# All of z by channel, half of the first expert weights loaded with the first pages, and work moved round the ends of the middle stages

## The chip, the cores and the metric

One Trainium2 chip, one core of it. The metric is device time in microseconds (us) for one execution of the whole program, as the median of the runs; the profile is of one execution of its own.

## What is computed

A long convolution with a computed filter, then a mixture of experts over every token of its result (float32 throughout):

```python
# x, v: (4, 10048, 128); pos_emb: (10048, 64)
h_filt = (np.maximum(pos_emb @ w1, 0) @ w2) * np.exp(-0.01 * pos)[:, None]
u  = x * v
Uf = np.fft.rfft(u, n=2 * S, axis=1)
Hf = np.fft.rfft(h_filt, n=2 * S, axis=0)
y  = np.fft.irfft(Uf * Hf[None], n=2 * S, axis=1)[:, :S]
x  = (x * y).reshape(B * S, D)                  # 40192 tokens of 128
# MoE: 4 groups of 4 experts, F = 1024; one group, then one expert, by argmax
g_idx = argmax(x @ w_group);  g_w = softmax(...)[g_idx]
e_idx = argmax(x[g_idx == g] @ w_expert[g]);  e_w = softmax(...)[e_idx]
out[token] = g_w * e_w * (np.maximum(x[token] @ w1[g, e], 0) @ w2[g, e])
```

## The kernel before

The transform is written as matrix products. A sequence is laid out as 128 positions by 79 (NB) blocks for each of the 128 channels (D). `dft_blocks` (L400) multiplies the folded input of three channels (`eo`) by a table and ScalarE (ACT) copies the result from PSUM to SBUF (L417) as the complex spectrum. That spectrum lives in two tiles: `z` holds the first 64 (KM) block frequencies, `zr` the other 15. In `z` the index order is [128, k, s, d] (s is the real or imaginary part, d the channel), in `zr` it is already [128, d, k, s]. Three steps use them:

- the *middle* of a batch, `middle` (L641) and `back` (L662), walks over the 79 frequencies two at a time (40 steps, k0 = 0, 2, ... 78): TensorE (PE) multiplies one frequency of all channels by a table (`dft_positions`, L489, result `psb`), VectorE (DVE) makes the two products with the filter's spectrum (`t0` L655, `t1` L658), GpSimd (POOL) adds and subtracts them into `y` (L656, L659), PE transforms back (L671, `pbp`), and ACT copies the result to `z` (L679) or `zr` (L682). `back` runs four steps (LAG) behind;
- the *next forward stage*, in which the inverse of the batch just done and the first transform of the next batch share one loop: PE transposes `zr` (L694, four channels in one) and `z` (L697, one channel each) through an identity, ACT copies the result (`tt`, L699), PE makes the inverse (L709, L730), DVE forms `yt` (L745) and `xy` (L747); beside them run `product` (L459), `fold` (L472) and `dft_blocks` (L406) of the next batch. `run_ahead` (L425) makes products and folds three parts (AHEAD) ahead of their use;
- at the end of the convolution a stage with the last inverse alone, whose `xy` is written into the space of `z`.

By the trace the stages are, in us: the filter to 119; the first transform of batch 0 to 175; middles at 175 to 249, 346 to 448, 553 to 658 and 772 to 875; shared stages at 249 to 346, 448 to 553 and 658 to 772; the last inverse to 945; then the choice of experts for the last batch and, from 969 to 2013, 164 pages of 256 tokens that each have one expert.

Tokens are sorted into pages as batches are done. For each batch, `chosen` (L800) computes the router's logits and the choice, and `ranked` (L857) counts (cnt L871, a small product pc on PE, L874), finds the page of every token and queues indirect DMAs on POOL: eight `clear`s (L387) of padding rows and 79 `put`s (L372) of tokens. Both are generators; the middle of the next batch calls them a step at a time (`next(routing)`), and the rest runs in the next shared stage. `scatter` (L324) sends queued clears and puts, a few for each step. A scheduler orders each engine's instructions, except that instructions marked `keep_in_program_order` stay as written, and `between`/`beyond` (L310, L317) hold POOL's indirect DMAs between marked POOL operations, here between one step's `y` L659 and the next.

In the ranking, four parts (h = 0 to 3) of 316 elements go through a scan, compares, a multiply by `dlt` (L960), an add (L963), a multiply by `oh` (L973) and a sum (L977). For batches 0 and 1, the three of h = 2 and 3 are on POOL (`w`, L956).

In the MoE part, each page loads its tokens (`xg`), and both halves of its expert's second weights (`ws`, L1236) from HBM. The first weights `m_w1` of all experts stay in SBUF as `mw0` and `mw1` (two halves of 4 MB); both are loaded in the last stage of the convolution, in 16 steps of 512 KB. `turn` (L1118) is one page's share of work: `high` (L1277) makes the high part of weights on ACT, `low` the rest, `first` (L1290) and `second` (L1310) are three products each, `leave` and `turn_back` bring the result to tokens (ys L1324, ptm L1331), `send` scatters it. What is left of `chosen` and `ranked` for the last batch runs beside the first pages.

## Time and profile before

| | us |
|---|---|
| runs, median (lowest to highest of 3) | 2032.28 (2028.17 to 2034.41) |
| the profiled execution, device time | 2026.35 |
| its span in the profile | 2024.4 |
| PE busy in the span | 1920.3 (95%) |
| DVE / ACT / POOL busy | 1607.3 / 1431.1 / 1302.2 |
| DMA, mean | 192 GB/s |

PE is busy nearly all the time, so a microsecond is to be had in two ways only: fewer or shorter PE instructions, or fewer of PE's idle stretches. The share of busy time is a mean over stages, so the stages are read one at a time, and PE's idle stretches are read with what ended them. The granted clock of PE (PEclk, 1.00 is 2.4 GHz, 0.50 is 1.2 GHz) is in the same rows. An fp32 product stands as two instructions in the trace (x4 is two frequencies), a transpose as one.

### The profile page before, as it was taken

What the parts mean: (1) busy time and instruction counts of PE and PEld (TensorE: products, weight loads), DVE (VectorE), ACT (ScalarE), POOL (GpSimd) and SP (SyncE); (2) the same over time, 40 slices, a digit from 0 to 9 for tenths busy, and PEclk for the clock granted to TensorE, in tenths of its full rate; (3) what the DMA queues carried; (4) which work ended last, traced back from release to release, by engine and by line L of the source; (5) the groups of instructions that cost most, each with busy time, mean ns of one, the idle gap of its engine ahead of it and who ended that gap; (6) DMA issues with size and microseconds to landing.
All of it is one profiled execution on the core that took longest, in us unless ns stands there. A gap on an engine that the chain in (4) does not pass through costs nothing.

```text
span 2024.4 us, 53259 instructions
## 1 busy us (share of the span) xinstructions
PE 1920.3 (95%) x17518; PEld 1768.2 (87%) x17518; DVE 1607.3 (79%) x3462; ACT 1431.1 (71%) x3395; POOL 1302.2 (64%) x1371
## 2 busy tenths in 40 slices
PE   8988999988998899988899999999999999999997
PEld 7867888767876787776799999999999999999997
DVE  5587766797669766883889998889999998888885
ACT  6663387427843585356787888888888888888886
POOL 3247700665798468966276777888888885555554
PEclk9999999989999899999899999999999999999999
DMA  4699967968998599877344445555555544443442
GB/s 140 213 270 259 291 178 210 334 191 224 278 333 262 159 249 342 287 249 257 107 147 143 143 152 147 158 192 157 163 157 157 161 142 127 133 130 124 123 124 67
DMA packets 258718, 388.72 MB, mean 192 GB/s; under 512 B 32679, under 2 KB 132754, under 8 KB 258432
## 3 DMA queue, kind: packets, MB, share of 16 engines
q1 hardware_dynamic: 225024, 317.84, 52.3%
q0 software_dynamic: 23904, 51.83, 7.3%
q10 hardware_dynamic: 9504, 15.54, 2.7%
q8 instruction: 142, 2.33, 0.5%
q14 instruction: 144, 1.18, 0.2%
HBM read 303.08 MB, written 83.04 MB: 191 GB/s over the span
## 4 chain that ended last, share of the span: by engine, by line
PE 70%; DVE 9%; issue 5%; DMA 4%; POOL 4%; ACT 4%; SPq 0%; ACTq 0%; DVEq 0%; POOLq 0%
PE py L1319 8%; PE py L1317 7%; PE py L1318 7%; PE ph L1298 7%; PE ph L1300 7%; PE ph L1299 7%; PE psb L489 6%; PE pbp L671 5%; PE psa L406 2%; PE po L730 2%; PE pt L697 2%; PE ptm L1331 2%; PE px L1255 2%; PE po L709 2%; PE ptr L812 2%
## 5 line engine op out<-in xcount | busy, mean ns | idle before, releaser
L1307 DVE SCALAR_TENSOR_TENSOR hl<-ph,hh 128x512 fp32r<-128x512 f32 x656 | 445.2, 684 | 93.3 <-ACT hh L1306 92.4
L1306 ACT ACTIVATE hh<-ph 128x512 fp32r<-128x512 f32 x656 | 393.8, 600 | 138.8 <-PE ph L1300 74.8
L372 POOL DMA_INDIRECT prow<-stg,adr x316 | 344.8, 1091 | 114.8 <-issue 54.8
L1343 POOL DMA_INDIRECT out<-os,to x328 | 344.8, 1051 | 91.5 <-issue 71.6
L1317 PE MATMUL py<-hh,wh 128*128 128x256 f32 x1312 | 399.4, 304 | 0.0
L1319 PE MATMUL py<-hh,wl 128*128 128x256 f32 x1312 | 373.9, 285 | 5.3 <-POOL wl L1287 5.3
L1298 PE MATMUL ph<-xh,wh 128*128 128x256 f32 x1312 | 374.3, 285 | 4.3 <-ACT wh L1280 2.5
L1300 PE MATMUL ph<-xh,wl 128*128 128x256 f32 x1312 | 374.0, 285 | 0.4 <-DVE wl L1287 0.4
L1299 PE MATMUL ph<-xl,wh 128*128 128x256 f32 x1312 | 373.8, 285 | 0.0
L1318 PE MATMUL py<-hl,wh 128*128 128x256 f32 x1312 | 371.8, 283 | 0.0
L1287 POOL TENSOR_TENSOR wl<-ws,wh 128x512 fp32r<-128x512 f32 x162 | 220.3, 1360 | 206.0 <-ACT wh L1280 205.0
L1319 PEld LDWEIGHTS py<-hh,wl 128*128 128x128 f32 x1312 | 252.0, 192 | 8.2 <-POOL wl L1287 8.2
L1298 PEld LDWEIGHTS ph<-xh,wh 128*128 128x128 f32 x1312 | 253.3, 193 | 5.0 <-ACT wh L1280 2.7
L1300 PEld LDWEIGHTS ph<-xh,wl 128*128 128x128 f32 x1312 | 253.5, 193 | 1.1 <-DVE wl L1287 0.8
L1299 PEld LDWEIGHTS ph<-xl,wh 128*128 128x128 f32 x1312 | 253.4, 193 | 0.1
L1318 PEld LDWEIGHTS py<-hl,wh 128*128 128x128 f32 x1312 | 253.4, 193 | 0.0
L1317 PEld LDWEIGHTS py<-hh,wh 128*128 128x128 f32 x1312 | 252.4, 192 | 0.0
L1287 DVE TENSOR_TENSOR wl<-mw,wh 128x512 fp32r<-128x512 f32 x328 | 236.7, 722 | 0.0
L656 POOL TENSOR_TENSOR y<-t 128x256 f32<-128x256 f32 (+1 forms) x160 | 119.7, 748 | 141.3 <-DVE t L655 135.7
L406 PE MATMUL psa<-fa,eo 96*64 96x158 f32 x2048 | 185.7, 310 | 23.2 <-DVE eo L472 11.2
L1280 ACT CAST wh<-mw 128x512 fp32r x328 | 205.8, 628 | 0.0
L1280 ACT CAST wh<-ws 128x512 fp32r<-128x512 f32 x328 | 204.7, 624 | 1.2 <-DMA ws<-m_w 1.2
(237 smaller groups left out, 4094.8 us busy)
## 6 DMA issues: line engine op xcount, KB each, us to landing
ws<-m_w SPq DMA_DIRECT2D x328, 256.0 KB
ht<-hspec SPq DMA_DIRECT2D x156, 256.0 KB
xv<-xv_in SPq DMA_DIRECT2D x131, 288.0 KB
bt<-c_b SPq DMA_DIRECT2D x95, 256.0 KB
xg<-prow SPq DMA_DIRECT2D x164, 130.0 KB
bp<-c_bp SPq DMA_DIRECT2D x76, 256.0 KB
stg<-xyd SPq DMA_DIRECT2D x76, 256.0 KB
xyd<-xy SPq DMA_DIRECT2D x57, 256.0 KB
```

The costliest lines, as they stand in the source:

```text
L372: ins = self.nc.gpsimd.indirect_dma_start(self.d["prow"], bass.IndirectOffsetOnAxis(ap=u.adr[:, t : t + 1], axis=0), u.rows[:, t - u.t0], ...
L1280: k.fix(k.nc.scalar.copy(hi, self.matrix(i, half, self.ea)))
L1287: ins = v.tensor_tensor(lo, self.matrix(i, half, self.ed), self.wh[i][half].bitcast(F32), ALU.subtract)
L1298: k.fix(nc.tensor.matmul(ph[:, j], wh, self.xh, start=True, stop=False))
L1299: k.fix(nc.tensor.matmul(ph[:, j], wh, self.xl, start=False, stop=False))
L1300: k.fix(nc.tensor.matmul(ph[:, j], wl, self.xh, start=False, stop=True))
L1306: k.fix(nc.scalar.activation(hh, ph, AF.Relu))
L1307: k.fix(nc.vector.scalar_tensor_tensor(hl, ph, 0.0, hh.bitcast(F32), ALU.max, ALU.subtract))
L1317: k.fix(nc.tensor.matmul(self.py, wh, self.hh[c], start=(c == 0), stop=False))
L1318: k.fix(nc.tensor.matmul(self.py, wh, self.hl[c], start=False, stop=False))
L1319: k.fix(nc.tensor.matmul(self.py, wl, self.hh[c], start=False, stop=(c == NC - 1)))
L1343: ins = k.nc.gpsimd.indirect_dma_start(k.d["out"], bass.IndirectOffsetOnAxis(ap=self.to[:, h : h + 1], axis=0), o[:, h], None, bounds_chec ...
```

## The change

- **Layout.** `z` becomes [128, d, k, s], as `zr` is. The transposes of `z` (L697) then read a channel's 128 values side by side instead of 512 bytes apart. `dft_positions` reads, for one frequency, pairs (s) that lie 512 bytes apart, instead of 256 values in a row. What it and `back` write to PSUM goes in the strided order that was used for `zr` only. ACT's copy of `dft_blocks` becomes contiguous on both sides.
- **Space.** The last batch's `xy` gets a tile of its own; `xo` has three buffers instead of four in the last stage.
- **Weights.** Only `mw0` is loaded in the last stage of the convolution. `mw1` is loaded in eight steps from MoE turn -2 on, and each of the first ten pages (EARLY) loads its own 256 KB of that half (`wf`).
- **Early products.** In the last four steps of a middle `run_ahead` makes four products and three folds of the next batch.
- **Later clears.** `scatter` in the middle no longer sends clears.
- **Ranking.** One more `yield` ahead of pc, for all but the last batch, and all of the ranking on DVE.

```diff
-        self.z = zp.tile([128, KM, 2, D], F32, name="z")
+        self.z = zp.tile([128, D, KM, 2], F32, name="z")
...
+        xyp = ctx.enter_context(tc.tile_pool(name="xy", bufs=1, reuse_waits="tile"))
         inner = ExitStack()
-        xyp = inner.enter_context(tc.tile_pool(name="xy", bufs=1, reuse_waits="tile"))
...
-                xy = self.z.rearrange("p k s d -> p (k s) d")[:, :NB]
-            elif b > 0:
+            if b > 0:
                 xy = xyp.tile([128, NB, D], F32, tag="xy", name=f"xy{b - 1}")
...
-                    self.scatter(i % 4 != 3)
+                    self.scatter(i % 4 != 3, False)
                     if i % 4 != 3 if i < 30 else i % 2:
                         next(routing, None)
+                    if i >= 36:
+                        self.run_ahead(b + 1, i - 36 - AHEAD - 1, made, folded)
...
-        return chain(*(self.moe_weights(pool, half) for half in range(2)))
+        return self.moe_weights(pool, 0)
...
-    def scatter(self, n):
+    def scatter(self, n, clear=True):
...
+            elif not clear:
+                break
...
-                self.by_channel(k0, ps)[:, i],
+                ps[:, i].rearrange("p s d -> p d s"),
                 bt[:, i],
-                self.frequency(k0 + i),
+                self.frequency(k0 + i, 1)[:, :, 0],
...
-                    src = self.z[:, :, :, d0 + s + i].rearrange("p k s -> p (k s)")
+                    src = self.z[:, d0 + s + i].rearrange("p k s -> p (k s)")
...
         yield
+        if b < self.nbat - 1:
+            yield
         pc = self.psr([128, 2, NE], "pc")
...
-            w = v if b >= self.nbat - 2 or h < 2 else nc.gpsimd
...
-            w.tensor_tensor(lt, lt, bc(dlt[:, es], 2, NB), ALU.mult)
+            v.tensor_tensor(lt, lt, bc(dlt[:, es], 2, NB), ALU.mult)
...
+        self.weights = self.moe_weights(
+            right.enter_context(tc.tile_pool(name="second", bufs=1, side="right", reuse_waits="tile")), 1
+        )
...
         p3.begin()
+        next(self.weights, None)
...
+        if self.q < EARLY:
+            self.wf = k.sp.tile([128, 512], F32, tag="wf", name="wf", bufs=3)
+            src = k.d["m_w1"][:, ds(es, 1), 512:1024]
+            k.tc.keep_in_program_order(nc.sync.dma_start(self.wf, src.rearrange("p e f -> p (e f)")))
...
+        if half and self.q < EARLY:
+            return self.wf
```

Three places show how the order of work moves. In the rows a name's number tells its buffers apart. The first place is the end of batch 1's middle (about 428 to 448 us in the trace of before), on POOL. Of before, from the first half of the last step's `y` on; `empty` to `prow` is a clear, and `y<-t1` is L659:

```order
L656 TENSOR_TENSOR y_5724<-t0_5725 128x128
L387 DMA prow<-empty_81,fidx_5548 13056x520
L659 TENSOR_TENSOR y_5636<-t1_5640 128x2x128
L387 DMA prow<-empty_81,fidx_5548 13056x520
L659 TENSOR_TENSOR y_5678<-t1_5682 128x2x128
L387 DMA prow<-empty_81,fidx_5548 13056x520
L659 TENSOR_TENSOR y_5706<-t1_5710 128x2x128
L387 DMA prow<-empty_81,fidx_5548 13056x520
L659 TENSOR_TENSOR y_5724<-t1_5728 128x128
```

Of after, the last three steps on POOL (after's line numbers: `y` is L657 and L660, a clear L391):

```order
L657 TENSOR_TENSOR y_5672<-t0_5673 128x2x128
L660 TENSOR_TENSOR y_5672<-t1_5676 128x2x128
L657 TENSOR_TENSOR y_5701<-t0_5702 128x2x128
L660 TENSOR_TENSOR y_5701<-t1_5705 128x2x128
L657 TENSOR_TENSOR y_5722<-t0_5723 128x128
L660 TENSOR_TENSOR y_5722<-t1_5726 128x128
L391 DMA prow<-empty_81,fidx_5584 13056x520 x8
```

The clears have moved behind the last `y`. On DVE at the same place, of before, the last two steps' products and the first rows of the ranking behind them:

```order
L655 TENSOR_TENSOR t0_5707<-psb_5703,ht_5697 128x512
L896 CAST npg_5524<-ni_5528 128x16
L658 TENSOR_TENSOR t1_5710<-psb_5703,ht_5697 128x512
L912 SCALAR_TENSOR_TENSOR end_5525<-ones_2987,used_68,npg_5524 128x16
L922 TENSOR_SCALAR lastp_5540<-npg_5524 128x16
L655 TENSOR_TENSOR t0_5725<-psb_5722,ht_5720 128x256
L913 TENSOR_TENSOR start_5534<-end_5525,npg_5524 128x16
L923 TENSOR_SCALAR lastp_5540<-lastp_5540 128x16
L658 TENSOR_TENSOR t1_5728<-psb_5722,ht_5720 128x256
L914 TENSOR_SCALAR base_5535<-start_5534 128x16
```

Of after on DVE, the end of what now stands ahead of those two steps (the block of 49 rows begins with the cast of npg, right behind t1_5676), and the two steps:

```order
L955 TENSOR_TENSOR lt_5683<-lt_5683,dlt_5624 128x316
L463 TENSOR_TENSOR xv_5686<-xv_5686 96x3x128
L476 TENSOR_TENSOR eo_5689<-xv_5664 96x384
L656 TENSOR_TENSOR t0_5702<-psb_5698,ht_5692 128x512
L659 TENSOR_TENSOR t1_5705<-psb_5698,ht_5692 128x512
L463 TENSOR_TENSOR xv_5712<-xv_5712 96x3x128
L476 TENSOR_TENSOR eo_5715<-xv_5686 96x384
L656 TENSOR_TENSOR t0_5723<-psb_5720,ht_5718 128x256
L659 TENSOR_TENSOR t1_5726<-psb_5720,ht_5718 128x256
L958 TENSOR_TENSOR f_5640<-f_5640,lt_5683 128x316
```

The ranking, which stood between and behind the last two steps' products, now stands ahead of them, with the early products of the next batch (`xv`, `eo`) among them. The second place is the same spot in batch 2's middle, where it is the same with 64 rows. The third is the start of the MoE part on DVE. Of before, the choice of experts of the last batch ahead of page 0's `hl` (L1307):

```order
L768 TENSOR_TENSOR ohe_14337<-dfe_14331,mxe_14329 128x64
L786 SCALAR_TENSOR_TENSOR smg_14030<-smg_14030,sme_14339 128x16
L791 TENSOR_TENSOR oh_13094<-ohe_14337,ohg_14028 128x16x16
L787 RECIPROCAL en_13095<-smg_14030 128x16
L760 TENSOR_REDUCE mxg_14641<-lg_13498 128x15
L762 TENSOR_TENSOR dfg_14643<-lg_13498,mxg_14641 128x60
L765 SCALAR_TENSOR_TENSOR dfg_14643<-dfg_14643,order_2996 128x60
L770 TENSOR_REDUCE smg_14651<-exg_14645 128x15
L766 TENSOR_REDUCE mxg_14641<-dfg_14643 128x15
L768 TENSOR_TENSOR ohg_14649<-dfg_14643,mxg_14641 128x60
L778 TENSOR_TENSOR pr_14653<-lg_13498,ohg_14649 128x240
L1307 SCALAR_TENSOR_TENSOR hl_13799<-ph_13785,hh_13798 128x512
```

Of after, the first piece of the same work between two `hl` and a `wl` of the pages:

```order
L1312 SCALAR_TENSOR_TENSOR hl_13666<-ph_13658,hh_13665 128x512
L777 TENSOR_REDUCE le_14334<-pr_14030 128x64
L754 TENSOR_REDUCE mxe_14336<-le_14334 128x16
L756 TENSOR_TENSOR dfe_14338<-le_14334,mxe_14336 128x64
L1292 TENSOR_TENSOR wl0_13673<-wf_13618,wh0_13669 128x512
```

What stood in one piece of 21 rows ahead of `hl` is split there into four pieces with pages' work between them.

## Rows read from the trace of the kernel before

**Rows 1.** Busy time by stage (columns in the first line; x is instructions).

```profile
core 0: us, PE busy (x) PEld busy (x) DVE busy (x) ACT busy (x) POOL busy (x), PEclk, DMA share, GB/s
249.00:346.00 97.00, 95.53 (x1441) 84.02 (x1442) 65.22 (x123) 81.15 (x215) 0.79 (x2) 1.00 0.67 183
...
346.00:448.00 102.00, 94.75 (x577) 75.61 (x577) 81.89 (x196) 40.05 (x93) 68.28 (x91) 0.95 0.87 283
...
448.00:553.00 105.00, 96.64 (x1440) 85.13 (x1440) 75.85 (x147) 81.80 (x214) 65.31 (x71) 0.97 0.85 233
...
658.00:772.00 114.00, 104.86 (x1422) 90.36 (x1422) 82.16 (x173) 80.94 (x210) 65.84 (x72) 0.91 0.78 214
...
875.00:945.00 70.00, 60.27 (x932) 51.95 (x930) 43.00 (x107) 46.47 (x87) 45.04 (x46) 1.00 0.81 274
...
969.00:1070.00 101.00, 94.36 (x742) 93.53 (x742) 89.43 (x224) 79.66 (x181) 53.89 (x48) 0.93 0.43 131
```

**Rows 2.** The weight loads of the transposes of z: group by line, count, busy us, mean ns.

```profile
L697 PEld LDWEIGHTS pt<-ident,z 128*128 128x128 f32 x512 | 82.3, 252 | 16.6 <-ACT tt L699 14.4 <-issue 2.0
```

**Rows 3.** PE in time, four transposes each (start us, us, work, count).

```profile
249.83 0.75 PE L697 MATMUL pt<-ident,z 128*128 128x128 f32 x4
...
952.46 0.60 PE L812 MATMUL ptr<-ident,z 128*128 128x128 f32 x4
```

**Rows 4.** PE in the first middle: psb and pbp, k0 below 64, then from 64.

```profile
215.11 1.03 PE L489 MATMUL psb<-z,bt 128*128 128x256 f32 x4
215.97 1.02 PE L671 MATMUL pbp<-y,bp 128*128 128x256 f32 x4
...
234.12 1.04 PE L489 MATMUL psb<-zr,bt 128*128 128x256 f32 x4
235.00 1.02 PE L671 MATMUL pbp<-y,bp 128*128 128x256 f32 x4
```

**Rows 5.** psb by group: count, busy us, mean ns of one.

```profile
L489 PE MATMUL psb<-z,bt 128*128 128x256 f32 x640 | 161.0, 385 | 9.5 <-DMA bt<-c_b 5.2 <-DVE hs L630 2.2 <-ACT zr L417 0.6
...
L489 PE MATMUL psb<-zr,bt 128*128 128x256 f32 x150 | 41.9, 402 | 0.6 <-DVE hs L630 0.4
```

**Rows 6.** PE in time at the end of batch 1's middle and after.

```profile
428.02 0.40 PE L874 MATMUL pc<-cnt,tri 128*128 128x16 f32 x2 [1.78 <-DVE cnt L871]
...
435.02 0.60 PE L489 MATMUL psb<-zr,bt 128*128 128x256 f32 x2
...
440.58 6.92 PE L671 MATMUL pbp<-y,bp 128*128 128x256 f32 x18 [4.96 <-POOL y L659]
...
459.16 1.06 PE L406 MATMUL psa<-fa,eo 96*64 96x158 f32 x6 [5.61 <-DVE eo L472]
```

**Rows 7.** POOL there: the first clear, and its wait.

```profile
438.68 1.08 POOL L387 DMA_INDIRECT prow<-empty,fidx  x1 [1.79 <-DVE oh L950]
```

**Rows 8.** DVE there: a t of the last step but one, and the next folds.

```profile
434.41 0.69 DVE L655 TENSOR_TENSOR t<-psb,ht 128x512 f32<-128x512 f32 x1 [0.27 <-POOL y L656]
...
458.56 1.95 DVE L472 TENSOR_TENSOR eo<-xv 96x384 f32<-96x384 f32 x4
```

**Rows 9.** Busy time while DVE ranks there.

```profile
436.77:447.13 10.36, 6.55 (x18) 5.24 (x18) 10.36 (x41) 1.80 (x4) 7.63 (x9) 0.67 0.58 187
```

**Rows 10.** A wait of PE at 658 to 772 (us in total, times, longest).

```profile
PE psa L406 <- DVE eo L472: 5.6, 2, 4.9
```

**Rows 11.** Multiply by dlt in the ranking, on POOL and on DVE.

```profile
L960 POOL TENSOR_TENSOR lt<-lt,dlt 128x316 f32<-128x316 f32 x4 | 4.3, 1081 | 6.6 <-DVE cur L1044 3.9 <-DVE lt L957 2.6
...
L960 DVE TENSOR_TENSOR lt<-lt,dlt 128x316 f32<-128x316 f32 x12 | 6.0, 503 | 0.0
```

**Rows 12.** The start of the MoE part: PE's wait, and 985 to 1005 us.

```profile
PE ptm L1331 <- ACT ys L1324: 4.0, 1, 4.0
...
985.00:1005.00 20.00, 16.02 (x115) 15.82 (x113) 18.57 (x51) 14.97 (x34) 7.17 (x7) 0.83 0.25 78
```

**Rows 13.** SP's queue at the first page.

```profile
971.33 2.59 SPq L1236 DMA_DIRECT2D ws<-m_w  x4
```

## What the change should do to the time

> **What bounds the kernel now.** I read the busy time by stage first [rows 1]. PE is busy 95.53 of 97 us in the first shared stage at a granted clock of 1.00, and from 92 to 93% in the middle of batch 1 and in two of the later shared stages; the last inverse is the loosest of the convolution's stages (60.27 of 70). So PE bounds nearly every stage, and each change is priced by what it takes off PE's own work or off PE's idle stretches. DVE is next (81.89 of 102 in a middle); ACT has slack there (40.05 of 102). Then I read what ended PE's idle stretches: at the end of a middle POOL's `y`, 4.96 us [rows 6]; in the stage behind it the folds `eo` on DVE, 5.61 us [rows 6], and 5.6 us again a batch later [rows 10]; at the start of the MoE part 4.0 us for `ys` [rows 12]. After such stretches the granted clock is under 1: 0.67 in 436.77 to 447.13 [rows 9], 0.91 over the stage from 658 [rows 1], 0.83 in 985 to 1005 [rows 12]. Below 1.00 a part of the stage ran at 1.2 GHz, so a gap costs more than its length.
>
> **Layout, the transposes.** There are 512 transposes of `z` [rows 2], 128 in each of four stages. Four of them take 0.75 us, and four whose source is contiguous take 0.60 [rows 3]: (0.75 - 0.60) / 4 = 0.0375 us each, 512 x 0.0375 = 19.2 us of PE, 4.8 us in each stage. What of it reaches the end: three of the stages are bound by PE for 92% and more of their time, and there I take 80%, 3 x 3.8 = 11.5 us, because ACT (81.15 of 97) and DVE stand close behind. In the last inverse PE idles 14% of the time, and I take half, 2.4 us. Together **-14 us**. Bounds: -19 (all of it) and -8 (half of the three, nothing of the last).
>
> **Layout, the products.** `psb` for k0 below 64 now reads pairs 512 bytes apart. The nearest row is `psb` from `zr`, which reads such pairs 128 bytes apart: 1.04 us for four against 1.03 [rows 4]. That is 2.5 ns each, x 640 instructions [rows 5] = +1.6 us. By group means it is 402 against 385 ns [rows 5], +10.9 us, but these durations overlap in the pipeline, so four in a row is the better reading. I take **+2**; bounds 0 and +11, and what the longer distance might add is a rival below. `back` writes PSUM strided in both cases: 1.02 against 1.02 [rows 4], 0. ACT's copies to `z` become runs of four values; ACT has 62 idle us in the middle of batch 1 [rows 1] to hide any growth. Without that cover, one copy later per step would reach PE only through the transposes at the stage's end: 0 to +1.
>
> A sentence of the Trainium skill (SBUF — State Buffer, the note on "cachelines" at the end of the part Door 1) speaks against this change: any non-contiguous access to PSUM slows matmuls significantly. It gives no figure to put in the sum. Both `psb` and `pbp` now write so for every k0, 128 more instructions per stage and kind. Rows 4 show the same pattern already, from k0 = 64 on, at 0.01 us for four; so the row decides, and the sum holds nothing for it.
>
> **Later clears and early products, end of batch 1's middle.** Before: PE ends the last `psb` at 435.02 + 0.60 = 435.62, then waits 4.96 us and needs 6.92 us for 18 `pbp` [rows 6]. Four take 1.02 us, about 0.22 each [rows 4], so 18 are 4 us of work in 11.9 us: 8 us lost. The cause is POOL: the first clear stands ahead of the last four `y` and waits 1.79 us for its list, which DVE makes in the ranking [rows 7]. After that comes the 5.61 us for the folds, which DVE makes only when it is through with that ranking (458.56 in [rows 8]). The change takes the clears out of there. But the order of DVE shows that it puts a block of 49 rows of ranking ahead of the products t0, t1 of the last two steps, so the wait is not gone, it changes hands: PE now waits for DVE. The price: such a stretch holds 41 instructions in 10.36 us, DVE full [rows 9]. Some of these are long only beside POOL's clears (I estimate 2 us), the block holds a product and a fold more of about 0.5 us each (1.95 us for four [rows 8]); I take 9 us, bounds 8 and 11. The t1 ahead of the block ends at about 434.0 (t0 of the next step starts at 434.41 in [rows 8], after a short wait that goes with the clears); the block then ends at 443.0. Two pairs of products (0.69 us each for a full step [rows 8], half that for the last) and two more early rows make 3 us, POOL's two halves of the last `y` and one `pbp` 1 us: PE ends the middle at 447 instead of 447.5. So the tail itself gives -0.5. The early folds are there when the next stage wants them, which takes away the 5.61 us; but the ranking that remains on DVE is longer (below), and I leave 2 us of waiting. Sum **-4**, bounds +1 (block 11 us and the wait back for half) and -10 (block hidden behind early `psa`).
>
> **The same for batch 2.** The block has 64 rows, by the same price per row about 11 us, where before the ranking stood behind the products: I take the tail 2.5 us longer. In the stage behind, the waits of 5.6 us for folds go [rows 10], and with them some of the time at 1.2 GHz (0.91 [rows 1]: if that stands for half speed in 18% of 114 us, 20 us ran slowly). Against it, DVE has the rest of the ranking. **-1.5**, bounds +4 and -12. For the middle of batch 3 the order stays: 0.
>
> **Ranking on DVE.** For batches 0 and 1, twelve instructions go from POOL to DVE; the multiply is 503 ns there against 1081 [rows 11]. At about 0.5 to 0.6 us each, six per batch are +3 us of DVE's time. The stage from 346 and those behind it have DVE at 66 to 80% [rows 1]; this is in the 2 us that I left above, and the next bound would be +3 each if DVE were full there. The added `yield` delays the count by one call, but PE's order around pc is the same in all three batches: its wait of 1.78 us [rows 6] stays, 0.
>
> **Weights, and the start of the MoE part.** In the last inverse SP issues eight loads of 512 KB fewer; DMA there is at 0.81 of its time [rows 1], PE waits for DVE and ACT, so 0. In the pages 4 MB more and ten times 256 KB come over about 100 us that move 131 GB/s now, 67 GB/s more; other stages move 283 [rows 1], so there is room. The first page: `wf` is the third load on SP's queue behind two `ws`, which takes 2.59 / 4 = 0.65 us per issue [rows 13], so it is asked for 1.3 us after the first `ws`, and the cast of it stands in ACT's queue ahead of `hh` of the next page; I charge +2.5 (bounds 0 and +8, the two first pages each waiting out a load). The gain here is not in the weights: the order of DVE splits the choice of experts of the last batch, which stood in one piece of 21 rows ahead of `hl`, and for which PE waits 4.0 us [rows 12]. Without it 4 us go, and of 20 us at a clock of 0.83 (34% of them at half speed, 3.4 us lost) I take 2. **-3.5** in all, bounds -8 and +8.
>
> **Space.** The own `xy` and one `xo` buffer less: `xo` is loaded by SP ahead of need, and the eight mw loads that shared the queue are gone, 0 to +2; taken as 0.
>
> **The sum.** -14 + 2 - 4 - 1.5 - 3.5 = -21. The profiled execution took 2026.35 us on a span of 2024.4; it gives 2005.35. It lies 5.93 under the median of 2032.28, and I forecast on the median: 2032.28 - 21 = **2011.3 us**. With all good halves of the small terms 2004, with the bad ones 2018.
>
> **Rivals.** First, *the distance of 512 bytes is what costs*, not the single hit in a line. For it: the old transposes are the only row that jumps 512 bytes, and they are the slow ones. Against it: `zr`'s pairs run at nearly full rate, but at 128 bytes. Then each `psb` pays for 128 jumps what a transpose pays, 37.5 ns, x 640 = 24 us, less the 2 in the sum: 2033, no change. If every value pays, it is twice that, +48: 2057, slower. It decides at 23 us, 36 ns for each of 640 instructions.
>
> The same note of the Trainium skill (SBUF — State Buffer, "cachelines") speaks against this rival: it counts hits in a line of 16 bytes, not the distance, and two in a line are enough for the full rate. By it the +2 of `psb` would be 0 and the time 2009; the trace agrees for pairs at 128 bytes [rows 4], and no row before shows pairs at 512.
>
> Second, *all waits go*: DVE's block hides behind the early `psa`, the stage behind batch 2 stays at full clock, the transposes give all 19: -19 + 2 - 10 - 12 - 7 = -46 at the most; half of the excess over my sum gives 1998 and all of it 1986. For it: PE does have early `psa` in its order there. Against it: these stand behind the `pbp` that wait.
>
> Third, *the wait only changes hands and the first pages pay*: the ends of the middles give nothing (0 and +4), `wf` and the mw1 loads put ahead of the tokens' loads in SP's order cost +7 at the first pages: -14 + 2 + 0 + 4 + 3.5 = -4.5: 2028; with milder terms 2020. For it: the DVE order. Against it: the bandwidth in hand.
>
> **How the numbers follow.** The forecast (2004 to 2018) has a chance of 0.55, the second rival (1986 to 2004) 0.17, the third (2018 to 2029) 0.17, the first 0.11: 0.05 at no change, 0.06 slower. A measurement of this kernel tells about 0.3%, 6 us, from no change, so faster begins below 2026.2: 0.55 + 0.17 + 0.12 = 0.84; same 0.05 + 0.05 = 0.10; slower 0.06. The range from 1994 to 2029 leaves out the lower half of the second rival and the first, 0.08 + 0.11 = 0.19.
>
> **What would show it.** Right: four transposes of `z` at 0.60 us; four `psb` below k0 = 64 at 1.04; no wait of PE for POOL's `y` at the end of batch 1's and 2's middles but one for t0 or t1 on DVE of 5 to 9 us; no 5.6 us wait for `eo`; no 4.0 us wait for `ys` at the MoE start, but 1 to 3 us for a `wh` or `wl` of `wf`. Wrong: `psb` at 1.15 us or more for four (first rival); stages behind the middles that lose what the tails gain; first pages that wait for `xg` or `ws`.

## The result

The changed kernel takes 2008.15 us (median of 4 runs, 2007.0 to 2012.78), the kernel before, beside it, 2031.82; the ratio is 0.990 (95% interval 0.9878 to 0.9922). By the two medians that is 23.7 us less, by the ratio some 20; I forecast 21 less and 2011.3 us. The profiled execution took 2008.12 us on a span of 2005.9.

The profile after, the busy time by stage; the columns are those of [rows 1], a stage starts with PE's first instruction of it:

```profile
core 0: us, PE busy (x) PEld busy (x) DVE busy (x) ACT busy (x) POOL busy (x), PEclk, DMA share, GB/s
247.00:339.50 92.50, 89.17 (x1431) 76.99 (x1430) 63.41 (x120) 76.92 (x210) 0.49 (x1) 1.00 0.67 184
339.50:443.80 104.30, 96.50 (x598) 75.78 (x596) 84.95 (x210) 41.62 (x98) 64.20 (x87) 0.95 0.84 274
443.80:540.10 96.30, 89.04 (x1425) 76.52 (x1423) 71.38 (x140) 77.49 (x211) 64.66 (x67) 1.00 0.91 252
540.10:654.60 114.50, 99.40 (x596) 75.34 (x596) 94.34 (x225) 41.76 (x98) 95.25 (x121) 0.93 0.84 280
654.60:750.10 95.50, 91.40 (x1429) 78.37 (x1427) 75.06 (x155) 77.29 (x210) 57.01 (x62) 0.98 0.91 252
853.30:923.50 70.20, 58.03 (x933) 48.19 (x934) 42.27 (x105) 44.95 (x87) 45.80 (x45) 0.98 0.69 214
946.50:1028.30 81.80, 77.66 (x611) 76.12 (x612) 73.91 (x182) 66.02 (x149) 44.81 (x40) 0.94 0.69 223
```

The first three shared stages (247, 443.8 and 654.6) have become shorter, the middles between them longer, above all the one from 540.1. Read the same way in both traces, from the first `psb`, the first transpose of `zr` or the first `px` to the next, and within the MoE part from a page's first `ptm`, the stages compare so (us; a negative difference is a gain):

| stage | before | after | difference |
|---|---|---|---|
| filter, then transform of batch 0 | 119.2 + 55.9 | 116.5 + 54.9 | -3.7 |
| middle 0, shared stage 1 | 73.8 + 97.0 | 75.6 + 92.6 | -2.6 |
| middle 1, shared stage 2 | 102.2 + 105.1 | 104.2 + 96.3 | -6.7 |
| middle 2, shared stage 3 | 104.0 + 115.9 | 114.5 + 95.5 | -10.0 |
| middle 3, last inverse, choice | 101.6 + 94.6 | 103.2 + 93.2 | +0.2 |
| pages 0 to 10 | 85.2 | 81.7 | -3.5 |
| pages 40 to 80 | 251.8 | 257.8 | +6.0 |
| other pages | 718.2 | 719.8 | +1.7 |

The sum is -18.6 us, 5 us less than the medians differ: the profiled execution of before (2026.35) lay that much under its median, and the one of after did not. So the table tells where the time went, and the medians how much it is in all.

The layout does in PE's rows what was forecast. Transposes of `z`, and `psb` and `pbp` in the first middle (compare [rows 3] and [rows 4]); columns: start, us, work, count:

```profile
211.17 1.03 PE L493 MATMUL psb<-z,bt 128*128 128x256 f32 x4
212.04 1.02 PE L669 MATMUL pbp<-y,bp 128*128 128x256 f32 x4
...
247.36 1.47 PE L691 MATMUL pt<-ident,z 128*128 128x128 f32 x12
...
450.87 1.04 PE L691 MATMUL pt<-ident,z 128*128 128x128 f32 x8
```

Twelve transposes take 1.47 us and eight 1.04, so one more costs (1.47 - 1.04) / 4 = 0.108 us. `psb` over pairs 512 bytes apart takes 1.03 us for four, as before: no loss at all. All transposes of `z` together, of before and of after (count, busy us and mean ns, then PE's idle time ahead of them):

```profile
L697 PE MATMUL pt<-ident,z 128*128 128x128 f32 x512 | 94.0, 322 | 6.5 <-ACT tt L699 6.5
L691 PE MATMUL pt<-ident,z 128*128 128x128 f32 x512 | 72.3, 280 | 14.3 <-ACT tt L693 14.1
```

PE is busy with them for 21.7 us less, and waits 7.6 us longer for ACT's copies `tt`. With the old layout in the changed kernel (the first experiment) it is 93.1 us and 6.5 us of waits, so both come from the layout.

The end of batch 1's middle, first PE, then DVE and POOL (compare [rows 6] to [rows 8]; the bracket is idle time ahead of the instruction and what ended it):

```profile
428.87 0.60 PE L493 MATMUL psb<-zr,bt 128*128 128x256 f32 x2
429.31 2.75 PE L669 MATMUL pbp<-y,bp 128*128 128x256 f32 x12
437.52 1.84 PE L410 MATMUL psa<-fa,eo 96*64 96x158 f32 x10 [5.46 <-DVE eo L476]
439.93 3.16 PE L669 MATMUL pbp<-y,bp 128*128 128x256 f32 x6 [0.56 <-POOL y L660]
...
427.99 0.24 DVE L892 CAST npg<-ni 128x16 f32<-128x16 int32 x1
...
436.92 0.55 DVE L476 TENSOR_TENSOR eo<-xv 96x384 f32<-96x384 f32 x1
437.39 0.68 DVE L656 TENSOR_TENSOR t<-psb,ht 128x512 f32<-128x512 f32 x1
...
438.15 0.72 POOL L657 TENSOR_TENSOR y<-t 128x256 f32<-128x256 f32 x1 [9.26 <-DVE t L656]
```

The clears are gone from between the `y`, and the block of ranking has come in their place: it starts at 427.99 on DVE and ends at 437.47, 9.5 us (I took 9), PE waits 5.46 us, and POOL 9.26 for the next `t`. A batch later it is the same with the longer block: its first and last rows on DVE, and PE's wait.

```profile
632.86 0.76 DVE L892 CAST npg<-ni 128x16 f32<-128x16 int32 x1
...
646.40 0.56 DVE L476 TENSOR_TENSOR eo<-xv 96x384 f32<-96x384 f32 x1
...
PE psa L410 <- DVE eo L476: 9.2, 2, 9.0
```

That block takes 14.1 us, where I took 11.

### The profile page after: what moved, and what is told of

Same layout as the page of the kernel before. It is cut to its first block, busy times and chain, and to the rows that moved or that the text cites. A ratio compares the mean times of both kernels' runs of the same rounds, so it can differ in the third digit from the quotient of the medians.

```text
span 2005.9 us, 53303 instructions
## 1 busy us (share of the span) xinstructions
PE 1896.0 (95%) x17518; PEld 1733.8 (86%) x17518; DVE 1624.4 (81%) x3478; ACT 1417.9 (71%) x3395; POOL 1303.4 (65%) x1355
## 4 chain that ended last, share of the span: by engine, by line
PE 64%; DVE 10%; DMA 6%; POOL 6%; ACT 4%; issue 4%; SPq 0%; ACTq 0%; DVEq 0%; POOLq 0%
PE py L1324 7%; PE ph L1303 7%; PE py L1322 7%; PE ph L1305 7%; PE py L1323 7%; PE ph L1304 7%; PE psb L493 5%; PE pbp L669 4%; PE po L724 2%; PE ptm L1336 2%; PE px L1258 2%; DMA xv<-xv_in 2%; PE ptr L806 2%; PE po L703 1%; DMA v<-xv_in 1%
## 5 line engine op out<-in xcount | busy, mean ns | idle before, releaser
L1322 PEld LDWEIGHTS py<-hh,wh 128*128 128x128 f32 x1312 | 251.7, 192 | 0.0
L657 POOL TENSOR_TENSOR y<-t 128x256 f32<-128x256 f32 (+1 forms) x160 | 121.6, 760 | 157.1 <-DVE t L656 154.2
L1285 ACT CAST wh<-mw 128x512 fp32r x318 | 199.9, 629 | 0.0
```

Source lines behind the costliest of these rows:

```text
L1285: k.fix(k.nc.scalar.copy(hi, self.matrix(i, half, self.ea)))
L1322: k.fix(nc.tensor.matmul(self.py, wh, self.hh[c], start=(c == 0), stop=False))
```

## The experiments

Each kernel is told as an edit of the changed kernel, or of the kernel before where it says so. The medians are read beside the runs of before on the same chip. The kernels came to several chips: before took 2031.82 us beside the changed kernel, 2030.23 beside the first four edits and 2033.49 beside the next four, so a difference of medians from two of these groups holds up to 3 us of the chips, and the ratio of each of these eight to before is known to 3 to 5 us. The last four (the ranking on DVE alone and those below it) ran on chips on which the kernel before took 2114 and 2125 us, so of them only ratios and single rows of undisturbed places are used.

**The old layout of z.**

```diff
-        self.z = zp.tile([128, D, KM, 2], F32, name="z")
+        self.z = zp.tile([128, KM, 2, D], F32, name="z")
...
-                    src = self.z[:, d0 + s + i].rearrange("p k s -> p (k s)")
+                    src = self.z[:, :, :, d0 + s + i].rearrange("p k s -> p (k s)")
```

> The changed kernel with the old layout of z ([128, k, s, d]) and everything else as changed. Theory of the prediction: the layout is the largest term, so this is 13 to 18 us slower than the changed kernel (2021 to 2026 us), four transposes of z take 0.75 us again, four psb below k0 = 64 stay at 1.03, and the filter and first transform, which came out 3.7 us shorter with no term in my sum, get that back because the copies from psa are strided again. Rival: most of the gain came from the waits at the ends of the middles, and the transposes only uncover other waits; then this is at most 6 us slower (2014 or less).

Measured: 2017.6 us, 0.9944 of before (0.9924 to 0.9964); the changed kernel is 9.5 us faster by medians. That lies between the theory (13 to 18) and the rival (6 or less). Its windows of the three shared stages and the last inverse, and PE's largest wait in the last inverse:

```profile
251.10:347.10 96.00, 94.32 (x1432) 83.13 (x1431) 63.67 (x120) 80.45 (x210) 0.46 (x1) 1.00 0.65 179
451.40:548.50 97.10, 94.15 (x1425) 82.63 (x1423) 71.37 (x140) 80.57 (x211) 64.44 (x67) 1.00 0.90 252
663.30:761.00 97.70, 95.68 (x1429) 83.94 (x1427) 75.28 (x155) 80.44 (x210) 58.59 (x62) 0.99 0.89 246
864.70:935.00 70.30, 63.38 (x939) 54.85 (x940) 42.82 (x104) 46.54 (x88) 44.70 (x45) 0.98 0.69 213
...
PE pt L701 <- ACT tt L703: 3.1, 7, 0.5
```

In stage 1 PE does 5.2 us less in the changed kernel (89.17 against 94.32), and the stage is 3.5 us shorter (92.5 against 96.0): 70% come through. In stage 2 PE does 5.1 us less and the stage is 0.8 us shorter, in stage 3 4.3 less and 2.2 shorter: 16% and 50%, each from one pair of traces. In the last inverse PE does 5.4 us less (58.03 against 63.38) and the stage is as long (70.2 against 70.3): nothing comes through. There the changed kernel's PE waits longer for ACT's copies of the transposes and for `yt`:

```profile
PE pt L691 <- ACT tt L693: 4.9, 7, 0.7
PE po L703 <- DVE yt L739: 2.6, 3, 1.5
```

The filter and the first transform are not explained by the layout: kernels whose work there is that of the changed one came to the transform of batch 0 at 116.5 to 119.8 us, which spans the 119.2 of before. So the -3.7 of the table lies within the spread between executions and can't be told from it. By these traces the layout is worth 3.5, 0.8 and 2.2 us in the three shared stages; where the rest of the 9.5 us lies isn't shown.

**No early products.**

```diff
-                    if i >= 36:
-                        self.run_ahead(b + 1, i - 36 - AHEAD - 1, made, folded)
```

> The changed kernel without the early products in the last four steps of a middle. By its order the block of 49 and 64 ranking rows ahead of t0, t1 of the last two steps goes with them. Theory (the wait changes hands): PE's waits of 5.5 and 9.0 us there go, the waits for eo of about 5 us in the two stages behind come back, with stretches at half clock; net between 2 us faster and 5 us slower than the changed kernel (2006 to 2013). Rival: the early products are what gained the 9 us that the pairs of batches 1 and 2 show beyond the transposes; then it is 7 to 10 us slower (2015 to 2018).

Measured: 1999.36 us, 0.9849 of before (0.983 to 0.9868), so 8.8 us *faster* than the changed kernel; outside what either theory expected, and against the sign of the rival. PE at the end of batch 1's middle:

```profile
431.58 4.04 PE L667 MATMUL pbp<-y,bp 128*128 128x256 f32 x18
436.15 0.55 PE L686 MATMUL pt<-ident,zr 128*128 128x128 f32 x3 [0.53 <-ACT zr L674]
...
445.38 4.85 PE L408 MATMUL psa<-fa,eo 96*64 96x158 f32 x44 [3.26 <-DVE eo L474]
```

The 18 `pbp` run in 4.04 us without a wait. Before, the same 18 took 6.92 us behind a wait of 4.96 [rows 6]. The wait for `eo` behind them comes back as 3.26 us, not as 5.61. So without the early products the end of the middle runs through, and the early products take that away: they save a wait of 3 us and make one of 5 to 9. By stages, the middles of batches 1 and 2 are 9.9 and 10.9 us shorter here than in the changed kernel (94.3 and 103.6), while shared stage 3 is 5.9 us longer (101.4).

**Ranking held back instead.** The early products stay, and the ranking isn't stepped on in the last four steps.

```diff
-                    if i % 4 != 3 if i < 30 else i % 2:
+                    if i % 4 != 3 if i < 30 else i % 2 and i < 36:
```

> The changed kernel, but the ranking is not stepped on in the last four steps of a middle (it goes on in the next stage). The early products stay, the block ahead of t0, t1 shrinks to 7 and 6 rows. Theory: the block of DVE is what PE waits for at the end of the middles, so 5.5 and 9.0 us and part of the half clock go, and 2 to 5 us come back where DVE ranks in the next stage: 6 to 11 us faster than the changed kernel (1997 to 2002). Rival: the ranking's DVE time only moves into the next stage and stalls PE there as long: 2006 to 2010.

Measured: 2011.39 us, 0.9908 (0.9891 to 0.9925), 3.2 us more than the changed kernel: no gain, as the rival has it (its range ends at 2010), but by another way. The two middles are 3.5 and 5.9 us shorter than in the changed kernel (100.7 and 108.6), though PE still waits for `y`:

```profile
PE pbp L669 <- POOL y L660: 4.7, 2, 3.4
```

The two stages behind lose 0.8 and 1.6 us. What is left over comes late: from the last inverse to the first page it takes 98.5 us instead of 93.2, and pages 80 to 160 take 504.2 instead of 501.8, with 142 of the tokens' puts left for the pages where the kernel before leaves 133.

**Clears back in the middle, without the added yield.** By the order either of the two alone keeps the clears behind the last `y`.

```diff
-                    self.scatter(i % 4 != 3, False)
+                    self.scatter(i % 4 != 3)
...
         yield
-        if b < self.nbat - 1:
-            yield
         pc = self.psr([128, 2, NE], "pc")
```

> The changed kernel with the clears sent in the middle again and without the added yield (either of the two alone keeps the clears behind the last y by the order; only both together bring clears back between the last y). Theory: with the early products DVE's block stands ahead of the last t0, t1 in any case and hides the clears, so it costs 0 to 4 us (2008 to 2012). Rival, as my prediction had it: the clears are the wait of 8 us at each of the two ends, and cost that again: 12 to 16 us slower (2020 to 2024).

Measured: 2010.35 us, 0.9904 (0.9886 to 0.9923), 2.2 us more than the changed kernel, the time that the theory expected. But the edit holds two things that work against each other. PE's waits at the end of batch 1's middle:

```profile
PE pbp L669 <- POOL y L660: 4.6, 3, 3.2
PE psa L410 <- DVE eo L476: 4.0, 1, 4.0
```

The wait for `y` is back beside that for the fold, and the middles of batches 1 and 2 are 5.1 and 3.1 us longer than in the changed kernel (109.3 and 117.6): the block on DVE doesn't hide the clears. Pages 40 to 80 take 252.3 us, as before, and not 257.8, which pays for most of it; the next run shows that this comes with the yield.

**No early products and no added yield**; the clears as changed.

```diff
-                    if i >= 36:
-                        self.run_ahead(b + 1, i - 36 - AHEAD - 1, made, folded)
...
-        if b < self.nbat - 1:
-            yield
         pc = self.psr([128, 2, NE], "pc")
```

> The changed kernel without the early products and without the added yield (clears stay out of the middle). In all kernels with later clears or the yield alone two to three more token puts are left for the MoE part, and pages 40 to 80 took 5 to 6 us longer; by its order this kernel has the puts of the kernel before. Theory: the 5 to 6 us there come from that, so this is 4 to 7 us faster than the changed kernel without early products alone (1993 to 1996 us; 0.982 of before). Rival: pages 40 to 80 differ for another reason (the weights, where the pages' loads lie), and it stays at 1998 to 2001 (0.985).

Measured: 1999.35 us, 0.9838 (0.9815 to 0.9861): the same median as without the early products alone, the rival's time, though on a chip where before took 3.3 us more; the ratios, 0.9838 against 0.9849, differ by 2 us, less than either is known to. But the theory's row is there. Pages 40 to 80 with the added yield (first row, no early products) and without it, and PE's waits for `wl` there in the same two kernels:

```profile
1208.20:1465.00 256.80, 251.13 (x2087) 248.44 (x2086) 235.65 (x441) 212.61 (x481) 217.91 (x201) 1.00 0.55 164
...
PE py L1322 <- POOL wl L1290: 5.5, 10, 1.3
```

```profile
1217.30:1469.10 251.80, 249.54 (x2086) 248.09 (x2085) 220.92 (x441) 212.59 (x481) 211.58 (x200) 1.00 0.55 165
...
PE py L1320 <- POOL wl L1288: 2.3, 5, 1.2
```

Without the yield POOL is busy 6.3 us and DVE 14.7 us less for the same pages, and PE waits less for `wl`. DVE's instructions are as many (441); 11 of its 14.7 us are the 40 casts of `to`, 0.53 us each on the mean against 0.80 with the yield. In this stretch 58 puts start against 59 with the yield; before and this kernel leave 133 puts for the pages, the changed one 136. In the four traces with 136 the part takes 256.8 to 257.8 us (257.3 in the one with 142), in the five with 133 251.7 to 252.3. All with 133 have no added yield, all with more have it, so the yield brings the 5 us; why three puts more make the casts so much longer isn't shown. The 5 us came back in the stages before, by 3.8 us in shared stage 3, 2.0 in shared stage 2 and 2.7 in the filter; the filter's part is the spread told above, that of the other two I can't tell from it.

**Clears back, no early products, no yield**: the layout, the weights, the space and the ranking alone. Beside the edit of the run before:

```diff
-                    self.scatter(i % 4 != 3, False)
+                    self.scatter(i % 4 != 3)
```

> The kernel of the run before this one, with the clears sent in the middle again: the layout, the weights, the space and the ranking on DVE alone. Theory (as predicted): clears ahead of the last y make PE wait at the ends of the middles of batches 1 and 2, 8 us each with the half clock behind: 8 to 16 us slower than without them (2002 to 2010). Rival: nothing else waits for those y in time, so clears cost nothing: 1993 to 1997.

Measured: 2004.8 us, 0.9859 (0.9837 to 0.988), 5.5 us more than the run before it. The time lies in the theory's range, the difference under its 8 to 16. The waits of before are back at 415 to 470:

```profile
PE pbp L667 <- POOL y L658: 5.0, 1, 5.0
PE psa L408 <- DVE eo L474: 4.3, 1, 4.3
```

The middle of batch 1 is 7.9 us longer than in the run before (102.2 against 94.3), as the theory has it, but that of batch 2 only 1.6 (104.9 against 103.3): at the second end the clears cost little.

**The weights alone**, in the kernel before.

```diff
-        return chain(*(self.moe_weights(pool, half) for half in range(2)))
+        return self.moe_weights(pool, 0)
...
+        next(self.weights, None)
...
+        if half and self.q < EARLY:
+            return self.wf
```

> The kernel before with the change of the weights alone (half of m_w1 in the last stage, the rest with the first pages, wf for ten pages). Theory of the prediction: the ranking at the MoE start is split by the scheduler because of this, the 4.0 us wait for ys goes: 2 to 5 us faster than before (0.9975 to 0.999 of it), the pages 40 to 80 as before. Rival: the split came with other parts of the change, and wf only costs: 0 to 6 us slower.

Measured: 2025.78 us, 0.9966 (0.9951 to 0.9981), 7.7 us by medians, a little more than the theory's 2 to 5, and 3.8 us to page 10 by the traces. PE's largest waits at the first pages:

```profile
PE ph L1309 <- ACT wh L1291: 4.8, 2, 2.7
PE ptm L1342 <- ACT ys L1335: 0.8, 2, 0.4
```

The 4.0 us for `ys` [rows 12] have become 0.8, and the wait for the first `wh`, 2.5 us in all in the kernel before, has become 4.8 in two pieces. The order of DVE at these pages is that of the changed kernel, so the split of the choice of experts comes with this part of the change alone. The other 4 us of the median don't show in the trace of that kernel, whose span is as long as that of before (2024.9 against 2024.4 us).

**Ranking on POOL again.**

```diff
+            w = v if b >= self.nbat - 2 or h < 2 else nc.gpsimd
...
-            v.tensor_tensor(f, f, lt, ALU.add)
+            w.tensor_tensor(f, f, lt, ALU.add)
```

> The changed kernel with the ranking's multiplies and adds of h = 2, 3 of batches 0 and 1 back on POOL; the block ahead of t0, t1 stays at 49 and 64 rows. Theory: DVE bounds the stages behind the middles, and it waited for POOL's results in before (4.6 and 1.7 us at 658 to 772), so this is 1 to 5 us slower than the changed kernel (2009 to 2013). Rival: the move only fills DVE, which is what PE waits for; then 2 to 4 us faster (2004 to 2006).

Measured: 2021.24 us, 0.9938 (0.9914 to 0.9962), 13.1 us slower than the changed kernel by medians of different chips, far more than the theory's 1 to 5; by the recorded ratios it is 8, and by the traces shared stages 2 and 3 are 5.3 and 6.0 us longer, 11.3 in all. PE's and DVE's waits in stage 2, and POOL's and DVE's rows at the place of DVE's second:

```profile
PE psa L410 <- DVE eo L476: 6.1, 2, 3.3
DVE other L973 <- POOL f L969: 9.8, 2, 5.9
...
460.10 4.00 POOL L391 DMA_INDIRECT prow<-empty,fidx  x1 [3.85 <-ACT zr L421]
464.40 0.98 POOL L391 DMA_INDIRECT prow<-empty,fidx  x1 [0.30 <-issue]
465.39 0.74 POOL L956 TENSOR_TENSOR lt<-lt,dlt 128x316 f32<-128x316 f32 x1
466.21 0.85 POOL L959 TENSOR_TENSOR f<-f,lt 128x316 f32<-128x316 f32 x1
467.22 1.01 POOL L391 DMA_INDIRECT prow<-empty,fidx  x1 [0.16 <-issue]
468.26 0.88 POOL L969 TENSOR_TENSOR f<-f,oh 128x316 f32<-128x316 f32 x1
...
469.17 0.69 DVE L973 TENSOR_REDUCE other<-f 128x79 f32<-128x316 f32 x1 [5.91 <-POOL f L969]
```

POOL's three steps are 2.5 us of work, but they stand in one queue with the clears, which the change has moved into this very stage, and a clear there waits 3.85 us for a copy on ACT and takes 4.00 itself. DVE waits 5.91 us for the last step, and the next folds stand behind that: PE's waits for `eo` grow from 3.3 to 6.1 us in stage 2 and from 0.5 to 4.4 in stage 3, and the granted clock falls from 1.00 to 0.95 and from 0.98 to 0.96. So with the later clears the ranking belongs on DVE.

**The ranking on DVE alone**, in the kernel before.

```diff
-            w = v if b >= self.nbat - 2 or h < 2 else nc.gpsimd
+            w = v
```

> The kernel before with the ranking on DVE alone. In the changed kernel this part was worth 13 us, where the prediction had 0 to 3 us of loss for it. Theory: DVE waits for POOL's slow ranking steps in the stages behind the middles, with puts of the same queue between them, and the folds come late behind that; so it helps in before too: 6 to 14 us faster than before (0.993 to 0.997). Rival: it is worth that much only where the early products have pushed the ranking ahead: 0 to 3 us (0.998 or more).

Measured: 0.9965 of before (0.9941 to 0.999), some 7 us on 2031: in the theory's range, also where the clears are still in the middle, though the interval (2 to 12 us) reaches into the rival's. Two earlier runs of one chip agree: the kernel with the layout, the weights, the space and the ranking on DVE (2004.8) is 21.0 us faster than that with the weights alone (2025.78), and the layout is 9.5 to 13 of that, which leaves 8 to 11.5 for the ranking and the space, without early products and with the clears in the middle.

**Early products without early folds**, then the same without the added yield (its two lines out, as above).

```diff
-                    if i >= 36:
-                        self.run_ahead(b + 1, i - 36 - AHEAD - 1, made, folded)
+                    if i >= 36 and b + 1 < self.nbat:
+                        made.append(self.product(b + 1, *groups(D, GD)[len(made)]))
```

> The changed kernel with only the early products kept: four products in the last four steps of a middle, no fold there (the folds come at the start of the next stage). By its order no block of ranking stands ahead of the last t0, t1 then (1 row and 2 to 5 where it was 49 and 64). Theory: it is the fold, not the product, that pulls the ranking ahead, so PE's waits of 5.5 and 9.0 us go as without the early products, and the wait for eo that was left there (3.3 us) gets shorter: 1996 to 2000 us. Rival: any early DVE work at this place delays t0, t1 and the ranking, and the time is that of the changed kernel or in the middle (2004 to 2009).

> As products_only, without the added yield, so that the puts are those of the kernel before and pages 40 to 80 take 252 us and not 257. Theory: 4 to 6 us faster than products_only (1991 to 1996), the fastest so far. Rival: as without early products at all, the yield makes no difference in the median, because what the pages save the stages before lose: within 2 us of products_only.

Measured: 0.9863 (0.9824 to 0.9901) and, without the yield, 0.9897 (0.9865 to 0.9929). The intervals are wide, and no gain over 0.985 is seen: the first time lies between the theory's range and the rival's, and the second theory's gain didn't show; on this chip pages 40 to 80 took 262 to 264 us with and without the yield. What the first theory says of the block can be read where the chip did not disturb, PE at the end of batch 1's middle:

```profile
433.88 4.04 PE L669 MATMUL pbp<-y,bp 128*128 128x256 f32 x18
438.44 0.55 PE L688 MATMUL pt<-ident,zr 128*128 128x128 f32 x3 [0.52 <-ACT zr L676]
```

No wait for the 18 `pbp`, as without any early product: at this place the early fold draws the ranking ahead, not the early product. Why the scheduler does that when a fold is there isn't shown.

**The old layout without early products**, the first two edits of this section together.

```diff
-        self.z = zp.tile([128, D, KM, 2], F32, name="z")
+        self.z = zp.tile([128, KM, 2, D], F32, name="z")
...
-                    if i >= 36:
-                        self.run_ahead(b + 1, i - 36 - AHEAD - 1, made, folded)
```

> The changed kernel without the early products and with the old layout of z; beside the run without the early products alone (0.985 of before, 1999 us) it gives the layout's worth a second time, where no block of ranking stands at the ends of the middles. Theory A: the transposes' 19 us are half hidden because ACT's copies of the transposes (tt) are late next, in any surroundings: 8 to 11 us slower than without the early products (0.989 to 0.991 of before). Theory B: it was the block on DVE and the half clock behind it that hid them, and without it they come through: 13 to 17 us slower (0.9915 to 0.9935).

Measured: 0.9915 (0.9881 to 0.9948), against 0.9849 with the new layout, on another chip: 13 us, with an interval that holds both theories. It doesn't settle whether the block on DVE hid a part of the transposes. In shared stage 1, which has neither block nor puts, it took 97.0 us against 93.6: the 3.4 us of the other pair again.

## Why the prediction was right, and where it wasn't

The time and the sign hold; that the sum does is partly luck, because large errors in it cancel: the early products cost 8.8 us where I counted on a gain, and the ranking gained some 11 where I had a loss or nothing.

- **Layout, -14 + 2 forecast, -9.5 measured.** The price of one transpose was right: 0.108 us is what 0.60 for four led to expect, and PE's own work falls by 4.3 to 5.4 us in a stage. `psb` costs 0 and not 2, so the first rival is out: 512 bytes between pairs cost nothing, as the rule on lines of 16 bytes in the Trainium skill (SBUF — State Buffer, "cachelines") has it. The sentence of the Trainium skill on PSUM (same page and note) isn't borne out here: the products written apart take 1.03 us for four, as those in a row did. The term that was mis-sized is the share that comes through: 70, 16 and 50% in the three shared stages where I took 80% of each, nothing in the last inverse where I took half. In the last inverse PE waits longer for ACT's copies of the transposes and for `yt`, and over all stages 7.6 us longer for these copies.
- **Ends of the middles, -4 and -1.5 forecast; the pairs of stages give -6.7 and -10.0, of which 0.9 and 2.5 are the layout, by the trace with the old one.** The mechanism was read rightly from the order: the wait changes hands, the block takes 9.5 us and PE waits 5.46 and 9.0 us for it ("5 to 9"). The sizes lie elsewhere than forecast: the middles became 2.0 and 10.5 us longer (-0.5 and +2.5 forecast, with 11 us for a block that took 14.1), the stages behind them 8.8 and 20.4 us shorter, and 0.6 and 3.6 us of PE's wait for `y` are left. What failed is the step that credits the early folds with the 5.61 us wait and the later clears with the tail's small gain. Taken one at a time, the later clears are worth 5.5 us by medians (7.9 us in the middle of batch 1 and 1.6 in that of batch 2 by the traces), the early products cost 8.8.
- **Ranking on DVE, 0 to +3 us each forecast; -11.3 by the two stages (-13.1 by medians) in the changed kernel, about -7 in the one before.** This is the step that was wrong by sign. I priced DVE's added busy time and left out what DVE waited for: POOL's steps in a queue with clears and puts. The 4.6 us of such waits in before I had seen and not put in the sum.
- **Added yield, 0 forecast.** PE's order round pc did stay (the wait is 1.74 us). But with the yield three puts more are left for the pages, and pages 40 to 80 take 5 to 6 us longer; the kernels with later clears and no yield show neither. I had no term for the MoE part beyond its start.
- **Start of the MoE part, -3.5 forecast, -3.5 measured to page 10**, and the weights alone do it. `wf` costs no more than the 2.5 us charged: the wait for the first `wh` grew by 0.9 us here (3.4 us in two pieces) and by 2.3 in the kernel with the weights alone.
- **Space, 0 forecast**: nothing in the traces speaks against it; it wasn't tried apart.

Two readings of [rows 1] were loose, without weight in the sum: DVE is busy 72 to 80% in the stages from 346 to 772, not 66 to 80, and the first transform of batch 0 (PE 46.76 of 55.9 us) is looser than the last inverse.

By medians the parts are: layout -9.5, ranking on DVE -13.1, weights -7.7, later clears -2.2 (together with the yield, with early products) to -5.5 (alone, without), early products +8.8. They add to -23.7 with the first value for the clears and to -27 with the second; the measured change is -23.7. That the first meets it to a tenth is chance: the medians come from several chips, each part is known to some 4 us, and some depend on each other (clears and ranking).

The changed kernel without the early products beats both kernels: 1999.36 us, 0.985 of before.

## What to carry to other kernels

Moving work ahead of its use in an engine's order is paid by whatever the scheduler then puts ahead of it: look in the order at what now stands before the critical instructions, and try the edit alone. When work leaves a slow engine, price not only its time on the new engine but also the queue in which it stood and who waited for its result. A share of PE's time that is taken away comes through only as far as the next engine lets it, and that differs from stage to stage: here 70, 16, 50 and 0%. And an edit that holds two parts can hide both: the clears and the yield were worth 8 and 5 us against each other, and the time showed 2.

## What the runs showed of the hardware

A single clear on POOL took 4.00 us where others in the same stage take 1.0. The changed kernel has one such in each of shared stages 2 and 3 (4.41 and 3.81 us), while the longest of before took 1.60; what makes them long isn't shown. And on two chips the kernel before took 2114 and 2125 us instead of some 2031. Most of the loss is in the shared stages that hold puts: early products without folds took 127.5 and 124.2 us for stages 2 and 3, the kernel without early products, on another chip, 97.1 and 101.4, while shared stage 1, which has no puts, took 93.6 us in both. The middles of batches 2 and 3 hold puts too and are not longer there (104.2 and 103.4 us against 103.6 and 105.5), so puts alone don't explain it. In stage 2 ACT had waits of up to 5.1 us that end with a remote event; the four runs on these chips have such waits, the other traces none:

```profile
ACT oo L733 <- remote: 13.3, 3, 5.1
```

What makes them wait on those chips isn't shown.
